# A decode layer's feed-forward tail: GELU, up and w_down taken out of the hand-synchronised section

## The chip, the core and the metric

The kernel runs on one core of one Trainium2 chip. A core has five engines with a queue of instructions each: TensorE (PE, matrix products), VectorE (DVE), ScalarE (ACT), GpSimd (POOL) and SyncE (SP), which here issues nearly all transfers. Sixteen DMA engines move data between the device memory (HBM) and the two on-chip memories' larger one, SBUF; matrix products land in PSUM, eight banks of 2 KB in each of 128 partitions. The metric is the time of one execution in microseconds, as the device measures it, median of the runs. The profiled execution is one further run whose instructions were recorded.

## The reference

One token goes through one layer of a transformer: layernorm, attention over a cache of 65,536 positions with 4 key/value heads and 32 query heads of 128, an output projection with a residual, and then a gated feed-forward block. Everything is bf16 in memory.

```python
def _A_ref(x, k_cache, v_cache, wq, wo):            # k_cache, v_cache: (1, 4, 65536, 128)
    q = (x @ wq).reshape(B, Sq, 32, 128)...
    p = _softmax(einsum("bhqd,bhkd->bhqk", q, k) * Dh ** -0.5, axis=-1)
    return einsum("bhqk,bhkd->bhqd", p, v)... @ wo  # wq: (1024, 4096), wo: (4096, 1024)

def _B_ref(x, w_gate, w_up, w_down):                # (1024, 3584), (1024, 3584), (3584, 1024)
    return (_gelu(x @ w_gate) * (x @ w_up)) @ w_down

x = A_x
h = x + _A_ref(_layernorm(x), A_k_cache, A_v_cache, A_wq, A_wo)
h2 = h + _B_ref(_layernorm(h), B_w_gate, B_w_up, B_w_down)
```

`_gelu` is the tanh approximation. The two caches are 134 MB; the weights of the feed-forward block are 7.3 MB each, 22 MB in all.

## The kernel before

All large data pass through one ring of four slots in SBUF (`ring`, 4 MB each; `slot(i, n)` is `n` slots from slot `i` on). The attention loop uses slots 2 and 3 for keys and 0 and 1 for values; after it, `wo` comes into slots 2 and 3, `w_gate` into 0 and 1 and `w_up` into 2 and 3. `w_down`'s 3584 rows are dealt out as 28 groups of 128 rows, one row of each group in each partition. The first FA = 16 groups (`wa`, 4 MB) overwrite slot 0, the next eight (`wb`, 2 MB) overwrite slot 1, and the last FZ = 4 groups have memory of their own, `w_end` (768 KB for three groups and 256 KB for the last). The first two take the place of `w_gate`, so they can be loaded only when gate's matmuls have read it. All these loads are issued by SyncE, on one DMA queue.

The feed-forward block goes in these steps. The normalised row stands in `hz` (8 columns of 128 values, each in a 32-wide tile of zeros). `ffn_in` (L557) loads a matrix and runs 64 matmuls (`wide_rows`, L325), eight for each column, four of them side by side in the four column groups of the array, into banks 0 and 1; VectorE transposes the two banks so that the 3584 results stand as 28 columns of 128 partitions (`rows_to_columns`, L332). This is done for gate, then GELU follows (L568 to L577: five small operations on VectorE around one Tanh on ScalarE, result `gl`), then the same for up, and `actz` gets gate times up (L600), each column in the middle of 63 zeros, so that a shifted 32-wide window puts the result on any row wanted.

The product with `w_down` accumulates in bank 2 and bank 7 (`d_ps`, `d_odd`). Its start value is the residual h: GpSimd spreads it out in `hb` (L585 to L589), and 16 fp32 matmuls put it into bank 2 (L590), half of which VectorE copies to bank 7 (L594). `wa`'s 16 groups are multiplied with 512 columns at a time into bank 6 (`down_wide`, L636, 32 matmuls); ScalarE copies that to SBUF and 8 matmuls add it to banks 2 and 7 (`add_wide`, L643). The other 12 groups go straight into banks 2 and 7, eight matmuls of 128 columns each (`down`, L621). Between the groups stand matmuls whose result nobody reads (`stay_busy`, L629). At the end VectorE and ScalarE copy rows 30 to 33 and 94 to 97 out and SyncE stores them (L669 to L672).

What sets the order? Nearly the whole kernel is written as a list of operations (`Flow`, L17), which `issue` (L82) turns into instructions with semaphores placed by hand; since `issue` makes every instruction, the profile gives them line 105. This list is issued inside a section (`tc.tile_critical`, L610), in which the framework (Tile) neither orders nor synchronises anything. Around a section the framework sets up an entry and an exit: SyncE lets the engines in; at the end each engine drains, SyncE waits for all of them (the join), and what depends on the section's data waits for that. Outside of sections the framework orders each engine's instructions itself, by their place in the text and by when it plans their inputs to be ready, and places the semaphores. An instruction that depends on nothing earlier can be put ahead of what precedes it in the text; `tc.keep_in_program_order` pins it behind the instruction before it on its engine. From L650 on, `tc.manual_schedule` keeps TensorE's instructions in the order of the text.

Before the change there are two sections. The first holds everything from the start to `actz`, and the loads of `wa` and `wb`. Outside stand the two loads of `w_end` (L613 to L619), pinned to their place, with semaphores of their own. The second section (L651 to L664) holds the filler, `wa`'s and `wb`'s groups and the fold; TensorE waits in it for the loads' semaphores. `w_end`'s groups stand outside again.

Of the kernel before, what the change touches and what calls it, by code (L numbers as in the profile page):

```python
# [8 lines left out]
ACT = mybir.ActivationFunctionType  # L9
ALU = mybir.AluOpType  # L10
# [108 lines left out]
def kernel(  # L119
# [13 lines left out]
    nc = tc.nc  # L133
    P = 128
    D = A_x.shape[-1]
# [4 lines left out]
    F = B_w_gate.shape[1]  # L140
    DC = D // P
    FC = F // P
# [11 lines left out]
    NT2 = Hkv * NH  # L154
    CW = DCH * CH * Dh
    NB = 512
# [25 lines left out]
    def sb(name, shape, dtype=F32):  # L182
        return const.tile(shape, dtype, name=name)
# [22 lines left out]
    def slot(i, n=1):  # L206
        return ring[:, i * CW:(i + n) * CW]
# [4 lines left out]
    s_qk, s_step = [tc.alloc_semaphore("from_pe_%d" % i) for i in range(2)]  # L212
    STEPS = 5
    k_sem = [tc.alloc_semaphore("k_landed_%d" % i) for i in range(DCH)]
    end_sem = [tc.alloc_semaphore("end_landed_%d" % i) for i in range(2)]


    XU = 32
# [106 lines left out]
    def wide_rows(banks, bkeys, rows_z, zkey, ci, blocks, wkeys, first, last):  # L325

        for t, w in enumerate(blocks):
            q = t % 4
            op("pe", "matmul", r=[zkey] + wkeys, w=[bkeys[t // 4]], out=banks[t // 4][32 * q:32 * q + 32, :], lhsT=rows_z[:, ci, :], rhs=w,
               start=first, stop=last, tile_position=(0, 32 * q))  # L330

    def rows_to_columns(banks, bkeys, key, order="p n -> p n", **sizes):  # L332

        w = [ps.shape[-1] for ps in banks]
        r = over(28672, [sum(w)])
        o = 0
        for ps, n, bk in zip(banks, w, bkeys):
            src = ps.rearrange(order, **sizes)
            op("dve", "transpose", r=[bk], w=[key], out=r[:, o:o + n].rearrange("p (e j) -> p e j", j=32) if sizes else r[:, o:o + n], in_=src)
            o += n  # L340
        return r[:, 0:o:32]
# [208 lines left out]
    def f_blocks(w_row):  # L550

        blocks = []
        for o, n in zip((0, P * FA), FW):
            blocks += [w_row[:, o + q * n:o + (q + 1) * n] for q in range(4)]
        return blocks

    def ffn_in(wmat, key, s0, b0):  # L557
        banks = [bank[b0 + i][:, 0:n] for i, n in enumerate(FW)]
        bkeys = ["B%d" % (b0 + i) for i in range(2)]
        rk = ["R%d" % s0, "R%d" % (s0 + 1)]  # L560
        wv = slot(s0, 2)[:, 0:DC * F].rearrange("p (c n) -> p c n", c=DC)
        f.dma("sp", wv, wmat.rearrange("(p c) n -> p c n", p=P), w=rk, sem=r_sem[s0], wait=[(s_step, STEPS * NT2 - 1)])
        for ci in range(DC):
            wide_rows(banks, bkeys, hz, "xz", ci, f_blocks(wv[:, ci, :]), rk, ci == 0, ci == DC - 1)
        return rows_to_columns(banks, bkeys, key, "p (j e) -> p e j", j=32)

    g_sb = ffn_in(B_w_gate, "g_r", 0, 0)
    t1 = sb("t1", [P, FC])  # L568
    op("dve", "tensor_tensor", r=["g_r"], w=["t1"], out=t1[:], in0=g_sb, in1=g_sb, op=ALU.mult)
    op("dve", "tensor_scalar", r=["t1"], w=["t1"], out=t1[:], in0=t1[:], scalar1=0.044715, scalar2=1.0, op0=ALU.mult, op1=ALU.add)  # L570
    op("dve", "tensor_tensor", r=["t1", "g_r"], w=["t1"], out=t1[:], in0=t1[:], in1=g_sb, op=ALU.mult)
    th = sb("th", [P, FC])
    op("act", "activation", r=["t1"], w=["th"], out=th[:], in_=t1[:], func=ACT.Tanh, scale=0.7978845608028654)
    hg = sb("hg", [P, FC])
    op("dve", "tensor_scalar", r=["g_r"], w=["hg"], out=hg[:], in0=g_sb, scalar1=0.5, scalar2=None, op0=ALU.mult)
    gl = sb("gl", [P, FC])
    op("dve", "scalar_tensor_tensor", r=["th", "hg"], w=["gl"], out=gl[:], in0=th[:], scalar=1.0, in1=hg[:], op0=ALU.add, op1=ALU.mult)  # L577


    OR = 8  # L580
    OB = D // OR
    orow = [30, 94, 31, 95, 32, 96, 33, 97]
    d_ps = bank[2][:, 0:OB]
    op("dve", "memset", w=["B2"], ap=d_ps, constant=0.0)
    hb = over(10240, [DC, P])  # L585
    op("pool", "memset", w=["hb"], ap=hb, constant=0.0)
    op("pool", "tensor_tensor", r=["h_col", "o_of"], w=["hb"], out=hb.rearrange("p j (b m) -> p j m b", b=2)[:, :, orow[0]:orow[0] + OR // 2, :],
       in0=h_col[:].unsqueeze(2).unsqueeze(3).to_broadcast([P, DC, OR // 2, 2]),
       in1=o_of[:].rearrange("p (a b) -> p a b", b=2).unsqueeze(1).to_broadcast([P, DC, OR // 2, 2]), op=ALU.mult)  # L589
    for j in range(DC):  # L590
        op("pe", "matmul", r=["hb", "sel16"], w=["B2"], out=d_ps[:, j:OB:DC], lhsT=hb[:, j, :], rhs=sel16[:],
           start=False, stop=False, skip_group_check=True)
    d_odd = bank[7][:, 0:OB]
    op("dve", "tensor_copy", r=["B2"], w=["B7"], out=d_odd[64:P, :], in_=d_ps[64:P, :])  # L594

    AZ = 31
    actz = over(16384, [FC, 2 * AZ + 2], BF16)
    op("pool", "memset", w=["actz"], ap=actz, constant=0.0)
    u_r = ffn_in(B_w_up, "u_r", 2, 0)
    op("dve", "tensor_tensor", r=["u_r", "gl", "actz"], w=["actz"], out=actz[:, :, AZ], in0=u_r, in1=gl[:], op=ALU.mult)  # L600

    wa = slot(0)[:, 0:FA * D].rearrange("p (e n) -> p e n", e=FA)
    wb = slot(1)[:, 0:FB * D].rearrange("p (e n) -> p e n", e=FB)
    wb_src = B_w_down[P * FA:F, :].rearrange("(p e) n -> p e n", p=P)
    parts = [(wa, 0, FA, f.dma("sp", wa, B_w_down[0:P * FA, :].rearrange("(p e) n -> p e n", p=P), after=["R0"], inc=(r_sem[0], 16)), r_sem[0])]
    e0 = 0
    w_body = wb_src[:, e0:FB - FZ, :]
    part = wb[:, e0:FB - FZ, :]
    parts.append((part, FA + e0, FB - FZ - e0, f.dma("sp", part, w_body, after=["R1"], inc=(r_sem[1], 16)), r_sem[1]))
    with tc.tile_critical(no_gpsimd_drain=True):  # L610
        f.issue()

    ends = []  # L613
    for i, (e1, e2) in enumerate(((FB - FZ, FB - 1), (FB - 1, FB))):
        d = nc.sync.dma_start(out=w_end[:, e1 - FB + FZ:e2 - FB + FZ, :], in_=wb_src[:, e1:e2, :])
        d.then_inc(end_sem[i], 16)
        tc.no_tile_sem_insts.add(d.ins.name)
        tc.keep_in_program_order(d)
        ends.append((d, e1, e2))  # L619

    def down(a_row, w_row, landed=None):  # L621
        for j in (0, 4, 1, 5, 2, 6, 3, 7):
            q, m = divmod(orow[j], 32)
            mm = nc.tensor.matmul((d_ps, d_odd)[q // 2][32 * q:32 * q + 32, :], lhsT=a_row[:, AZ - m:AZ - m + 32], rhs=w_row[:, j * OB:(j + 1) * OB],  # L624
                             start=False, stop=False, skip_group_check=True, tile_position=(0, 32 * q))
            if landed is not None:
                tc.declare_no_dep(mm.ins, landed.ins, query=mybir.DependencyQuery.ANY, reason="TensorE waits for the load's own semaphore ahead of it")

    def stay_busy(n):  # L629
        for i in range(n):  # L630
            nc.tensor.matmul(bank[5][:], lhsT=qs[:, 0, 0, 0:P], rhs=qs[:, 1 + i % 3].rearrange("p s c -> p (s c)")[:, 0:NB], start=True, stop=True)
# [4 lines left out]
    def down_wide(a_row, w_row, e, n):  # L636
        for h in range(DS):
            q = 2 * (e % 2) + h
            mm = nc.tensor.matmul(e_ps[32 * q:32 * q + 32, :], lhsT=a_row[:, AZ:AZ + 32], rhs=w_row[:, h * NB:(h + 1) * NB],
                             start=(e < 2), stop=(e >= n - 2), tile_position=(0, 32 * q))  # L640
        return mm

    def add_wide():  # L643
        for c in range(C4):
# [1 line left out]
            nc.tensor.matmul((d_ps, d_odd)[h][64 * h:64 * h + 64, :], lhsT=fold[:, 1 - c // 2:65 - c // 2], rhs=e_sb[:, c * OB:(c + 1) * OB],  # L646
                             start=False, stop=False, skip_group_check=True, tile_position=(0, 64 * h))

    (w_rows, a0, n, at, sem), (w_rows2, a2, n2, at2, sem2) = parts
    ctx.enter_context(tc.manual_schedule(engines={mybir.EngineType.PE}))  # L650
    with tc.tile_critical(no_gpsimd_drain=True):  # L651
        stay_busy(4)
        nc.tensor.wait_ge(sem, at)
        for e in range(n):
            mm = down_wide(actz[:, a0 + e, :], w_rows[:, e, :], e, n)
        mm.then_inc(s_step, 1)
        nc.scalar.wait_ge(s_step, STEPS * NT2 + 1)
        nc.scalar.copy(out=e_sb[:], in_=e_ps[:]).then_inc(from_act, 1)
        stay_busy(3)
        nc.tensor.wait_ge(from_act, 1)  # L660
        add_wide()
        nc.tensor.wait_ge(sem2, at2)
        for e in range(n2):
            down(actz[:, a2 + e, :], w_rows2[:, e, :])  # L664
    for i, (d, e1, e2) in enumerate(ends):
        nc.tensor.wait_ge(end_sem[i], 16)
        for e in range(e1, e2):
            down(actz[:, FA + e, :], w_end[:, e - FB + FZ, :], d)
    h2 = sb("h2", [P, 2, OB], BF16)  # L669
    nc.vector.tensor_copy(out=h2[0:64, 0, :], in_=d_ps[0:64, :])  # L670
    nc.scalar.copy(out=h2[0:64, 1, :], in_=d_odd[64:P, :])  # L671
# [31 lines left out]
```

## Time and profile before

| what | value |
|---|---|
| time, median of 3 runs (lowest, highest) | 409.39 us (409.34, 409.49) |
| profiled execution: its own time | 409.36 us |
| profiled execution: span from first to last instruction | 407.6 us |
| read from HBM | 173.02 MB, 424 GB/s over the span |
| DMA queue of SyncE, share of 16 engines | 98.6% |
| busy: PE, DVE, ACT, POOL | 56%, 49%, 10%, 4% |
| mean granted TensorE clock | 0.803 |

Times in the profile are microseconds from the first instruction. In a line of the chain or of the instructions in order of time, the first figure is the start and the second the length; "out<-in" names what is written and read, "x64" is the number of instructions merged in the line, and the bracket gives the idle time of the engine before it and what ended it. SPq is SyncE's queue, which issues transfers. "Time to landing" runs from a transfer's issue to the semaphore that says that all of it has arrived. In a table of stretches each engine has its busy time and, in brackets, its instructions; after the engines come the granted TensorE clock (1.00 is full), the share of the DMA engines and GB/s.

### The profile page before, as it was taken

How to read it: one execution, taken by the hardware profiler on the slowest of the kernel's cores; microseconds unless marked ns; L12 is line 12 of the kernel's file. 1: busy time of each engine (PE TensorE's matmuls, PEld its weight loads, DVE VectorE, ACT ScalarE, POOL GpSimd, SP SyncE). 2: the span in 40 equal slices, each digit the busy share in tenths (PEclk: the TensorE clock that was granted, in tenths of full speed). 3: DMA queues.
4: the chain of work that ended last, by engine and by line, in shares of the span. 5: the costliest groups of instructions: out<-in, count | busy, mean ns of one | idle time of the engine just before them, and what ended most of it. 6: DMA issues, size and time to landing. Idle time of an engine off the chain costs nothing. (4 is left out here: it accounts for less than half of the span.)

```text
span 407.6 us, 3713 instructions
## 1 busy us (share of the span) xinstructions
PE 227.4 (56%) x1557; PEld 100.0 (25%) x1558; DVE 201.0 (49%) x160; ACT 40.0 (10%) x142; POOL 16.6 (4%) x27
## 2 busy tenths in 40 slices
PE   0432854674677468715873686468456737634156
PEld 0110322231232133202321332233122213222123
DVE  2226860894079328734962686188509940121110
ACT  1000003000300130030003000300040021000000
POOL 4210000001000000010000001000000000030000
PEclk9975896899569778968896689589968986566688
DMA  8999999999999999999999999999999999999995
GB/s 360 412 453 420 441 434 418 453 418 432 434 460 418 412 445 469 418 412 418 495 418 389 441 431 447 412 466 412 418 450 457 424 405 428 457 445 435 396 415 220
DMA packets 4958, 173.10 MB, mean 425 GB/s; under 512 B 596, under 2 KB 600, under 8 KB 856
## 3 DMA queue, kind: packets, MB, share of 16 engines
q1 hardware_dynamic: 4904, 173.02, 98.6%
q8 instruction: 4, 0.07, 0.1%
q14 instruction: 2, 0.02, 0.0%
q10 hardware_dynamic: 48, 0.00, 0.0%
HBM read 173.02 MB, written 0.00 MB: 424 GB/s over the span
## 5 line engine op out<-in xcount | busy, mean ns | idle before, releaser
L105 DVE STREAM_TRANSPOSE ktb<-ring 128x4096 f32<-128x4096 f32 x32 | 141.1, 4417 | 74.9 <-DMA ring<-in_A_k_cache_dram 74.9
L450 PE MATMUL bank<-ktb,qs 128*128 128x512 bf16 x512 | 129.6, 412 | 55.1 <-PEq L436 55.1
L450 PEld LDWEIGHTS bank<-ktb,qs 128*128 128x128 bf16 x512 | 51.0, 103 | 130.5 <-issue 83.2
L462 PE MATMUL bank<-ring,pt 128*32 128x512 bf16 x512 | 44.8, 527 | 36.5 <-PEq L436 36.5
L105 ACT ACTIVATE pt<-sc,nb 128x256 bf16<-128x256 f32 x64 | 31.5, 494 | 256.6 <-DVE nb L105 256.6
L105 DVE STREAM_TRANSPOSE sc<-bank 128x512 f32<-128x512 f32 x32 | 22.2, 695 | 35.9 <-PE bank L450 35.9
L462 PEld LDWEIGHTS bank<-ring,pt 128*32 128x32 bf16 x512 | 18.9, 127 | 59.3 <-issue 55.6
L105 PE MATMUL bank<-ring,xz 128*32 128x512 bf16 (+1 forms) x192 | 16.6, 521 | 22.6 <-DMA ring<-in_B_w_gate_dram 8.3
L105 DVE STREAM_TRANSPOSE ktb<-bank 128x512 f32<-128x512 f32 (+1 forms) x6 | 4.0, 672 | 34.3 <-PE bank L105 34.0
L105 DVE TENSOR_REDUCE mx<-sc 128x8 f32<-128x2048 f32 x8 | 18.3, 2286 | 0.3
L454 PE MATMUL bank<-ident_f,mx 128*8 128x128 f32 x8 | 2.5, 307 | 25.8 <-PEq L436 25.8
L105 POOL COPY qs<-qsel 128x512 bf16<-128x512 bf16 x4 | 5.3, 1326 | 233.6 <-PE bank L450 219.6
L105 PEld LDWEIGHTS bank<-ring,xz 128*32 128x32 bf16 x192 | 6.5, 128 | 31.3 <-issue 14.5
L105 ACT ACTIVATION_READ_ACCUMULATOR pt<-sc,nb 128x1 f32 x64 | 12.0, 187 | 0.0
L471 PE MATMUL bank<-sel,acc_sb 128*128 128x8 f32 x64 | 8.2, 255 | 6.2 <-PEq L436 6.2
L471 PEld LDWEIGHTS bank<-sel,acc_sb 128*128 128x128 f32 x64 | 7.7, 191 | 10.0 <-issue 10.0
L105 ACT COPY acc_sb<-bank 128x512 f32<-128x512 f32 x8 | 4.7, 586 | 47.4 <-PE bank L462 47.4
L105 PE MATMUL bank<-ring,ktb 128*32 128x512 bf16 x64 | 7.0, 614 | 1.9 <-DMA ring<-in_A_wo_dram 1.2
L454 PEld LDWEIGHTS bank<-ident_f,mx 128*8 128x8 f32 x8 | 0.7, 83 | 29.5 <-issue 29.5
L456 PE MATMUL bank<-diag,ones_f 8*128 8x8 f32 x16 | 3.5, 287 | 5.7 <-PEq L436 5.7
L105 POOL MEMSET ktb<- 128x1024 bf16 (+2 forms) x3 | 3.5, 1164 | 74.9 <-PE bank L450 74.9
L105 DVE TENSOR_TENSOR h_col<-bank,x_col 128x8 f32<-128x8 f32 x1 | 0.2, 167 | 11.4 <-PE bank L105 11.4
(96 smaller groups left out, 61.4 us busy)
## 6 DMA issues: line engine op xcount, KB each, us to landing
ring<-in_A_k_cache_dram SPq DMA_DIRECT2D x16, 4096.0 KB, 24.8
ring<-in_A_wq_dram SPq DMA_DIRECT2D x2, 4096.0 KB, 16.5
ring<-in_A_wo_dram SPq DMA_DIRECT2D x2, 4096.0 KB, 25.5
ring<-in_B_w_gate_dram SPq DMA_DIRECT2D x1, 7168.0 KB, 26.6
ring<-in_B_w_up_dram SPq DMA_DIRECT2D x1, 7168.0 KB, 30.4
ring<-in_B_w_down_dram SPq DMA_DIRECT2D x1, 4096.0 KB, 21.8
ring<-in_B_w_down_dram SPq DMA_DIRECT2D x1, 2048.0 KB, 26.3
w_end<-in_B_w_down_dram SPq DMA_DIRECT2D x1, 768.0 KB, 27.5
```

The source lines that it names most:

```text
L105: ins = getattr(self.eng[e], o["call"])(**o["kw"])
L450: m = nc.tensor.matmul(bank[c][:], lhsT=qs[:, jt].rearrange("p s c -> p (s c)")[:, s * P:(s + 1) * P], rhs=mv[:, :, J, :, u], start=(s == ...
L454: nc.tensor.transpose(out=mxT_ps, in_=mx1[:], identity=ident_f[:]).then_inc(s_step, 1)
L456: nc.tensor.matmul(bc_ps, lhsT=ones_f[0:rep, :], rhs=diag[:], start=True, stop=True).then_inc(s_step, 1)
L462: m = nc.tensor.matmul(acc[32 * q:32 * q + 32, :], lhsT=pt[:, c, n, :, :].rearrange("p h s -> p (h s)"), rhs=v_sb[:, c, :, n, :], start=(c ...
L471: m = nc.tensor.matmul(o_ps, lhsT=acc_sb[:, u * Dh:(u + 1) * Dh], rhs=sel[:, u:SQ:NS], start=(u == 0), stop=(u == NS - 1))
```

## The change

The first section ends with gate's matmuls. The load of `w_up` stays in it, behind gate's (`ffn_load`). What follows stands outside of sections: the four loads of `w_down` in the order `wa`, `wb`, first and second `w_end`, each with a semaphore of its own (`end_sem` has four now), none with a wait or a signal of the framework's, and none pinned to its place; the operations on h; GELU; up's matmuls; and all of `w_down`'s groups. The loads form a group with a fence on TensorE (`waits_itself`), so that the framework lets TensorE read what they bring without waiting; TensorE waits by `wait_ge` on the loads' semaphores instead. Since up's load was issued in the section, TensorE's wait for its landing stands in a small section of its own. The memory views, the sizes and the matmuls are the same. The filler is four matmuls behind up's, as before, and two instead of three while ScalarE copies `wa`'s result.

```diff
-    def ffn_in(wmat, key, s0, b0):
+    def ffn_load(wmat, s0):
         ...
-        return rows_to_columns(banks, bkeys, key, "p (j e) -> p e j", j=32)
+        return wv, rk
+
+    f_banks = [bank[i][:, 0:n] for i, n in enumerate(FW)]
+    gate_w, rk = ffn_load(B_w_gate, 0)
+    for ci in range(DC):
+        wide_rows(f_banks, ["B0", "B1"], hz, "xz", ci, f_blocks(gate_w[:, ci, :]), rk, ci == 0, ci == DC - 1)
+    up_w, _ = ffn_load(B_w_up, 2)
+    with tc.tile_critical(no_gpsimd_drain=True):
+        f.issue()
+
+    ctx.enter_context(tc.manual_schedule(engines={mybir.EngineType.PE}))
     ...
+    loads = [(wa, B_w_down[0:P * FA, :].rearrange("(p e) n -> p e n", p=P)), (wb[:, 0:FM, :], wb_src[:, 0:FM, :]),
+             (w_end[:, 0:FZ - 1, :], wb_src[:, FM:FB - 1, :]), (w_end[:, FZ - 1:FZ, :], wb_src[:, FB - 1:FB, :])]
+    for (dst, src), sem in zip(loads, end_sem):
+        d = nc.sync.dma_start(out=dst, in_=src)
+        d.then_inc(sem, 16)
+        tc.no_tile_sem_insts.add(d.ins.name)
+        tc.add_to_no_dep_group("loads", d.ins)
+    waits_itself = nc.tensor.nop()
+    tc.declare_fence(waits_itself.ins, group="loads")
     ...
-    parts = [(wa, 0, FA, f.dma("sp", wa, B_w_down[0:P * FA, :].rearrange("(p e) n -> p e n", p=P), after=["R0"], inc=(r_sem[0], 16)), r_sem[0])]
     ...
-    with tc.tile_critical(no_gpsimd_drain=True):
-        f.issue()
-
-    ends = []
-    for i, (e1, e2) in enumerate(((FB - FZ, FB - 1), (FB - 1, FB))):
-        d = nc.sync.dma_start(out=w_end[:, e1 - FB + FZ:e2 - FB + FZ, :], in_=wb_src[:, e1:e2, :])
-        d.then_inc(end_sem[i], 16)
-        tc.no_tile_sem_insts.add(d.ins.name)
-        tc.keep_in_program_order(d)
-        ends.append((d, e1, e2))
     ...
+    nc.gpsimd.memset(hb, 0.0)
+    nc.gpsimd.tensor_tensor(out=hb..., in0=h_col..., in1=o_of..., op=ALU.mult)
+    nc.gpsimd.memset(actz, 0.0)
     ...
+    nc.vector.memset(d_ps, 0.0)
+    g_sb = columns(over(28672, [sum(FW)]))
     ...
+    for j in range(DC):
+        nc.tensor.matmul(d_ps[:, j:OB:DC], lhsT=hb[:, j, :], rhs=sel16[:], start=False, stop=False, skip_group_check=True)
+    d_odd = bank[7][:, 0:OB]
+    nc.vector.tensor_copy(out=d_odd[64:P, :], in_=d_ps[64:P, :])
+
     with tc.tile_critical(no_gpsimd_drain=True):
+        nc.tensor.wait_ge(r_sem[2], f.landed[r_sem[2].name])
+    for ci in range(DC):
+        ...
+    u_r = columns(over(28672, [sum(FW)]))
+    nc.vector.tensor_tensor(out=actz[:, :, AZ], in0=u_r, in1=gl[:], op=ALU.mult)
     ...
-    (w_rows, a0, n, at, sem), (w_rows2, a2, n2, at2, sem2) = parts
-    ctx.enter_context(tc.manual_schedule(engines={mybir.EngineType.PE}))
-    with tc.tile_critical(no_gpsimd_drain=True):
-        stay_busy(4)
-        nc.tensor.wait_ge(sem, at)
     ...
-    for i, (d, e1, e2) in enumerate(ends):
-        nc.tensor.wait_ge(end_sem[i], 16)
-        for e in range(e1, e2):
-            down(actz[:, FA + e, :], w_end[:, e - FB + FZ, :], d)
+    stay_busy(4)
+    nc.tensor.wait_ge(end_sem[0], 16)
+    for e in range(FA):
+        down_wide(actz[:, e, :], wa[:, e, :], e, FA)
+    nc.scalar.copy(out=e_sb[:], in_=e_ps[:])
+    stay_busy(2)
+    add_wide()
+    e = FA
+    for (dst, _), sem in list(zip(loads, end_sem))[1:]:
+        nc.tensor.wait_ge(sem, 16)
+        for i in range(dst.shape[1]):
+            down(actz[:, e, :], dst[:, i, :])
+            e += 1
```

More of the change, by code (lines that the diff above doesn't have):

```diff
@@ L214 @@
     k_sem = [tc.alloc_semaphore("k_landed_%d" % i) for i in range(DCH)]
-    end_sem = [tc.alloc_semaphore("end_landed_%d" % i) for i in range(2)]
+    end_sem = [tc.alloc_semaphore("end_landed_%d" % i) for i in range(4)]
     XU = 32
@@ L555, in f_blocks @@
         return blocks
-    def ffn_in(wmat, key, s0, b0):
-        banks = [bank[b0 + i][:, 0:n] for i, n in enumerate(FW)]
-        bkeys = ["B%d" % (b0 + i) for i in range(2)]
+    def ffn_load(wmat, s0):
         rk = ["R%d" % s0, "R%d" % (s0 + 1)]
@@ L562, in ffn_in @@
         f.dma("sp", wv, wmat.rearrange("(p c) n -> p c n", p=P), w=rk, sem=r_sem[s0], wait=[(s_step, STEPS * NT2 - 1)])
-        for ci in range(DC):
-            wide_rows(banks, bkeys, hz, "xz", ci, f_blocks(wv[:, ci, :]), rk, ci == 0, ci == DC - 1)
-        return rows_to_columns(banks, bkeys, key, "p (j e) -> p e j", j=32)
[L567 to L577, printed above, removed]
+        return wv, rk
[7 more added lines that the diff above has]
+    ctx.enter_context(tc.manual_schedule(engines={mybir.EngineType.PE}))
+    wa = slot(0)[:, 0:FA * D].rearrange("p (e n) -> p e n", e=FA)
+    wb = slot(1)[:, 0:FB * D].rearrange("p (e n) -> p e n", e=FB)
+    wb_src = B_w_down[P * FA:F, :].rearrange("(p e) n -> p e n", p=P)
+    FM = FB - FZ
+    loads = [(wa, B_w_down[0:P * FA, :].rearrange("(p e) n -> p e n", p=P)), (wb[:, 0:FM, :], wb_src[:, 0:FM, :]),
[7 more added lines that the diff above has]
+    tc.declare_fence(waits_itself.ins, group="loads")
     OR = 8
@@ L583 @@
     d_ps = bank[2][:, 0:OB]
-    op("dve", "memset", w=["B2"], ap=d_ps, constant=0.0)
     hb = over(10240, [DC, P])
[L586 to L594, printed above, removed]
     AZ = 31
     actz = over(16384, [FC, 2 * AZ + 2], BF16)
-    op("pool", "memset", w=["actz"], ap=actz, constant=0.0)
-    u_r = ffn_in(B_w_up, "u_r", 2, 0)
-    op("dve", "tensor_tensor", r=["u_r", "gl", "actz"], w=["actz"], out=actz[:, :, AZ], in0=u_r, in1=gl[:], op=ALU.mult)
@@ L602 @@
-    wa = slot(0)[:, 0:FA * D].rearrange("p (e n) -> p e n", e=FA)
-    wb = slot(1)[:, 0:FB * D].rearrange("p (e n) -> p e n", e=FB)
-    wb_src = B_w_down[P * FA:F, :].rearrange("(p e) n -> p e n", p=P)
-    parts = [(wa, 0, FA, f.dma("sp", wa, B_w_down[0:P * FA, :].rearrange("(p e) n -> p e n", p=P), after=["R0"], inc=(r_sem[0], 16)), r_sem[0])]
[L606 to L609, printed above, removed]
@@ L610 @@
-    with tc.tile_critical(no_gpsimd_drain=True):
-        f.issue()
-    ends = []
-    for i, (e1, e2) in enumerate(((FB - FZ, FB - 1), (FB - 1, FB))):
-        d = nc.sync.dma_start(out=w_end[:, e1 - FB + FZ:e2 - FB + FZ, :], in_=wb_src[:, e1:e2, :])
-        d.then_inc(end_sem[i], 16)
-        tc.no_tile_sem_insts.add(d.ins.name)
-        tc.keep_in_program_order(d)
-        ends.append((d, e1, e2))
-    def down(a_row, w_row, landed=None):
+    nc.gpsimd.memset(hb, 0.0)
+    nc.gpsimd.tensor_tensor(out=hb.rearrange("p j (b m) -> p j m b", b=2)[:, :, orow[0]:orow[0] + OR // 2, :],
+                            in0=h_col[:].unsqueeze(2).unsqueeze(3).to_broadcast([P, DC, OR // 2, 2]),
+                            in1=o_of[:].rearrange("p (a b) -> p a b", b=2).unsqueeze(1).to_broadcast([P, DC, OR // 2, 2]), op=ALU.mult)
@@ new lines, with columns @@
+    nc.gpsimd.memset(actz, 0.0)
+    def columns(r):
+        o = 0
+        for ps, n in zip(f_banks, FW):
+            nc.vector.transpose(out=r[:, o:o + n].rearrange("p (e j) -> p e j", j=32), in_=ps.rearrange("p (j e) -> p e j", j=32))
+            o += n
+        return r[:, 0:o:32]
+    nc.vector.memset(d_ps, 0.0)
+    g_sb = columns(over(28672, [sum(FW)]))
+    t1, th, hg, gl = [sb(n, [P, FC]) for n in ("t1", "th", "hg", "gl")]
+    nc.vector.tensor_tensor(out=t1[:], in0=g_sb, in1=g_sb, op=ALU.mult)
@@ new lines @@
+    nc.vector.tensor_scalar(out=t1[:], in0=t1[:], scalar1=0.044715, scalar2=1.0, op0=ALU.mult, op1=ALU.add)
+    nc.vector.tensor_tensor(out=t1[:], in0=t1[:], in1=g_sb, op=ALU.mult)
+    nc.scalar.activation(out=th[:], in_=t1[:], func=ACT.Tanh, scale=0.7978845608028654)
+    nc.vector.tensor_scalar(out=hg[:], in0=g_sb, scalar1=0.5, scalar2=None, op0=ALU.mult)
+    nc.vector.scalar_tensor_tensor(out=gl[:], in0=th[:], scalar=1.0, in1=hg[:], op0=ALU.add, op1=ALU.mult)
+    for j in range(DC):
+        nc.tensor.matmul(d_ps[:, j:OB:DC], lhsT=hb[:, j, :], rhs=sel16[:], start=False, stop=False, skip_group_check=True)
@@ new lines @@
+    d_odd = bank[7][:, 0:OB]
+    nc.vector.tensor_copy(out=d_odd[64:P, :], in_=d_ps[64:P, :])
+    with tc.tile_critical(no_gpsimd_drain=True):
+        nc.tensor.wait_ge(r_sem[2], f.landed[r_sem[2].name])
+    for ci in range(DC):
+        for t, w in enumerate(f_blocks(up_w[:, ci, :])):
+            q = t % 4
+            nc.tensor.matmul(f_banks[t // 4][32 * q:32 * q + 32, :], lhsT=hz[:, ci, :], rhs=w, start=(ci == 0), stop=(ci == DC - 1),
+                             tile_position=(0, 32 * q))
@@ L622, in down @@
+    u_r = columns(over(28672, [sum(FW)]))
+    nc.vector.tensor_tensor(out=actz[:, :, AZ], in0=u_r, in1=gl[:], op=ALU.mult)
+    def down(a_row, w_row):
         for j in (0, 4, 1, 5, 2, 6, 3, 7):
             q, m = divmod(orow[j], 32)
-            mm = nc.tensor.matmul((d_ps, d_odd)[q // 2][32 * q:32 * q + 32, :], lhsT=a_row[:, AZ - m:AZ - m + 32], rhs=w_row[:, j * OB:(j + 1) * OB],
+            nc.tensor.matmul((d_ps, d_odd)[q // 2][32 * q:32 * q + 32, :], lhsT=a_row[:, AZ - m:AZ - m + 32], rhs=w_row[:, j * OB:(j + 1) * OB],
@@ L625, in down @@
                              start=False, stop=False, skip_group_check=True, tile_position=(0, 32 * q))
-            if landed is not None:
-                tc.declare_no_dep(mm.ins, landed.ins, query=mybir.DependencyQuery.ANY, reason="TensorE waits for the load's own semaphore ahead of it")
     def stay_busy(n):
@@ L638, in down_wide @@
             q = 2 * (e % 2) + h
-            mm = nc.tensor.matmul(e_ps[32 * q:32 * q + 32, :], lhsT=a_row[:, AZ:AZ + 32], rhs=w_row[:, h * NB:(h + 1) * NB],
+            nc.tensor.matmul(e_ps[32 * q:32 * q + 32, :], lhsT=a_row[:, AZ:AZ + 32], rhs=w_row[:, h * NB:(h + 1) * NB],
                              start=(e < 2), stop=(e >= n - 2), tile_position=(0, 32 * q))
-        return mm
     def add_wide():
@@ L647, in add_wide @@
                              start=False, stop=False, skip_group_check=True, tile_position=(0, 64 * h))
-    (w_rows, a0, n, at, sem), (w_rows2, a2, n2, at2, sem2) = parts
-    ctx.enter_context(tc.manual_schedule(engines={mybir.EngineType.PE}))
-    with tc.tile_critical(no_gpsimd_drain=True):
-        stay_busy(4)
-        nc.tensor.wait_ge(sem, at)
[L654 to L664, printed above, removed]
-    for i, (d, e1, e2) in enumerate(ends):
-        nc.tensor.wait_ge(end_sem[i], 16)
-        for e in range(e1, e2):
-            down(actz[:, FA + e, :], w_end[:, e - FB + FZ, :], d)
+    stay_busy(4)
[11 more added lines that the diff above has]
+            e += 1
     h2 = sb("h2", [P, 2, OB], BF16)
```

## The prediction

> **What bounds the kernel now.** I read the page's strip of DMA load first, then the chain that ended last, then SyncE's own instructions and waits, then TensorE's instructions in order of time for the last 20 us, and last the stretches with the granted clock.
>
> ```profile
> DMA  8999999999999999999999999999999999999995
> q1 hardware_dynamic: 4904, 173.02, 98.6%
> ```
>
> The DMA engines hold work from start to end, on one queue (98.6% of the span). The time is therefore the bytes, plus what is left to do after the last byte. The chain shows that rest:
>
> ```profile
> 344.09 26.63 DMA ring<-in_B_w_gate_dram
> ...
> 376.66 27.47 DMA w_end<-in_B_w_down_dram
> 404.13 0.14 issue
> 404.27 0.52 PE bank L624 x24
> 404.79 0.01 issue
> 404.79 0.35 PE bank L624 x8
> 405.14 0.02 issue
> 405.17 0.26 ACT h L671
> ```
>
> Only the last 1 MB of w_down (`w_end`, two loads) has matmuls behind its landing, and they are few: 24, then 8. PE ends at 405.14, 0.35 us after the last landing.
>
> ```profile
> 375.61 0.81 SPq L105 DMA_DIRECT2D ring<-in_B_w_down_dram  x2
> 376.66 18.16 SPq L615 DMA_DIRECT2D w_end<-in_B_w_down_dram  x2
> SPq L610 <- DVEq L610: 17.3, 1, 17.3
> ```
>
> The first two lines are SyncE's, the third its waits. The four w_down loads leave in the order `wa`, `wb`, first `w_end`, second `w_end`. The two `w_end` issues lie 17.8 us apart (376.66 and 394.49): between them SyncE sits 17.3 us in the join that ends the section, waiting for VectorE. So a load that depends on nothing in the section was put ahead of the section's join, and the next one behind it.
>
> ```profile
> 387.70 4.82 PE L105 MATMUL bank<-ring,xz 128*32 128x512 bf16 x64 [7.46 <-DMA ring<-in_B_w_up_dram]
> 395.47 0.81 PE L631 MATMUL bank<-qs 128*128 128x512 bf16 x3 [2.95 <-SPq L651]
> 397.41 3.24 PE L639 MATMUL bank<-ring,ktb 128*32 128x512 bf16 x32 [1.13 <-DMA ring<-in_B_w_down_dram]
> 400.58 1.14 PE L631 MATMUL bank<-qs 128*128 128x512 bf16 x3
> 401.65 0.66 PE L646 MATMUL bank<-e_sb,fold 128*64 128x128 f32 x8
> 402.31 1.08 PE L624 MATMUL bank<-ring,ktb 128*32 128x128 bf16 x64
> 404.27 0.82 PE L624 MATMUL bank<-w_end,ktb 128*32 128x128 bf16 x32 [0.88 <-DMA w_end<-in_B_w_down_dram]
> ```
>
> This is the staircase of landings that TensorE follows. From issue plus time to landing: up 387.7 (357.27 + 30.4), `wa` 397.41 (375.61 + 21.8), `wb` 402.28 (375.98 + 26.3), `w_end` 404.13 and 404.79 (394.49 + 10.3). PE waits at each step, so it has slack everywhere but after the last byte.
>
> **The change part by part**, on the profiled execution (span 407.6, its own time 409.36, against the median 409.39 of the three runs).
>
> The section now ends after gate's last matmul (375.59), not after VectorE's `actz` (394.20). The old end gives the price of a join: from VectorE's end to the next load 0.29 us (394.49), to TensorE's next instruction 1.04 us (395.24). So `wa` and `wb` leave at about 375.9 to 376.4 instead of 375.61 and 375.98. Queued behind the join on SyncE are these two loads and the entry of the next section. The up load keeps the queue fed until 387.69; cover 11 us; cost 0.
>
> GELU on VectorE starts at 376.6 (375.59 + 1.04) instead of 375.45: memset 0.17, transposes 1.40, six small operations and Tanh about 1.2, done near 379.4. GpSimd's two memsets and one product (0.95 + 0.31 + 1.59 us), which ran from 363.3 under gate's load, now start after the join and end by 379.5. The 16 fp32 matmuls of h (1.96 us) end by 379.9, the copy (0.31) by 380.2. If the two engines were made to take turns on the shared tile, everything ends near 383. All of it lies under up's landing; cover 4.7 to 7.5 us; cost 0. One more table load on ScalarE (1.28 us, the one row of its kind) would also fit.
>
> The new section around the wait for up has an entry and an exit. The nearest rows are that 1.04 us hop, and the 0.85 us between 403.39 and 404.24 at the old second section's end, which a landing ended. From nothing to 1.9 us, then; I take 1.04, the row that no landing cut short. Up then ends near 393.6 and `actz` near 395.2, against `wa`'s landing at 397.41: cover 2.2 us, and 1.3 at the upper end. Cost 0.
>
> TensorE's filler: four now directly behind up, then two instead of three (0.38 us each). They end before `wa` lands, and the fold waits for ScalarE's copy (401.27) anyway. The second section's end goes; the idle time there (403.39 to 404.24) was ended by `w_end`'s landing, so this gains 0 to 0.1.
>
> The loads are what is left. All four lose their pin to program order. `wa` and `wb` overwrite slots that gate's matmuls read, so they stay behind the join. The two `w_end` loads write memory that nothing earlier touches, so nothing holds them behind `wa`. They may go into the gap ahead of the join, which on SyncE now opens right after up's issue (357.6), or ahead of the whole section. Either way their 1 MB moves in front of `wa`. The queue's bytes and end stay the same (404.79), but the order of landing changes. The last 1 MB took 2.51 us (404.79 - 402.28), so `wa` lands at 399.92 and `wb` is the last to land, at 404.79. `wa`'s rows end at 403.16 (3.24), the copy at 403.78 (0.04 + 0.58), the fold at 404.44 to 404.8 (0.66, with or without the 0.37 that lay ahead of it): just hidden. Behind the last byte there are now 64 + 32 matmuls instead of 8. The rate is (1.08 - 0.22)/63 = 13.7 ns in the first group and (0.52 - 0.22)/23 = 13.0 in the second, 0.22 us being one matmul's length. With 13.5 ns: 95 x 13.5 + 220 = 1.50 us, so PE ends at 406.29 instead of 405.14: **+1.15 us, 410.5**. The ends for this case: 13.0 ns a matmul and none lost at the switch gives +1.1; 17 ns (1.08/64, with each group's latency counted again) +1.5.
>
> The clock: the stretches show where it stands as the staircase ends.
>
> ```profile
> 394.50:397.90 3.40, 1.30 (x15) 0.57 (x20) 0.00 (x0) 0.00 (x0) 0.00 (x0) 0.99 0.94 400
> 397.90:401.30 3.40, 3.40 (x30) 1.11 (x23) 0.00 (x0) 0.58 (x1) 0.00 (x0) 0.51 0.96 402
> 401.30:404.70 3.40, 2.52 (x98) 1.69 (x96) 0.00 (x0) 0.00 (x0) 0.00 (x0) 1.00 0.47 186
> ```
>
> The seventh figure after the length is the granted clock. 1.30 us of work in 3.4 us led to half clock in the next stretch, 3.40 us of work to full clock again. The filler now comes right behind up, so TensorE idles from about 394.5 to 399.9 and starts `wa`'s rows cold, as it mostly does now (0.51). By 404.8 it has worked 403.2 - 399.9 and the fold, so I take full clock for the tail.
>
> [...]
>
> **The rivals.** First, order kept: the framework issues the loads as written, `w_end` last. Then the landings stay and PE ends at 405.14; with both `w_end` loads landed before 404.79 at best 0.2 us less. 409.4, no change. For it: the second `w_end` load did leave behind the join. Against it: the first did not, and the old text pinned both to their place. It decides as soon as neither `w_end` load passes `wa`.
>
> Second, only one passes, as now: the gap took one load. Then `wb` lands at 404.13, and from 404.27 96 matmuls take 1.50: 405.77, +0.63, 410.0.
>
> Third, TensorE late or cold. Cold: 96 matmuls at 27 ns from 404.8, +2.45, 411.8. Late: `wa` and `wb` behind the new section's join in SyncE's queue would leave after up's landing, near 388.2; with some 1.7 us to the first bytes (the output's store, issued at 405.49 in a span that ends at 407.6, bounds it) the queue stands empty 2.2 us, 411.6. For: SyncE takes joins in order. Against: the loads come first in the text and are ready 11 us earlier.
>
> Fourth, faster: in stretches of 0.6 us from 402.4 the DMA share falls to 0.54, 0.30, 0.16 and 0.01, as some engines finish early; 0.6 x (0.46 + 0.70 + 0.84 + 0.99) = 1.8 us of idle share. If another order of sizes levelled this, 407.6. No row shows that the order sets it.
>
> **How the numbers follow.** Both loads ahead 0.38 (410.5; own range 410.3 to 410.9), one ahead 0.12 (410.0), order kept 0.28 (409.4), late or cold 0.14 (411.6 to 411.8), faster 0.08. A measurement of this kernel can tell about 0.2%, 0.8 us. Slower: 0.38 + 0.13, and a quarter of the one-ahead case, 0.54. Same: 0.28, the rest of one ahead and a little of the late case, 0.38. Faster 0.08. The range from 409.1 (order kept, with 0.2 gained) to 411.8 (cold) leaves out the faster case and a little above. The forecast is 410.5.
>
> **What would show it.** In SyncE's list both `w_end` issues ahead of `wa`'s, near 358 or near 1; `wa`'s rows start near 399.9; the last chain ends in `wb`'s landing with some 96 short matmuls behind it. In the order kept, `w_end` still ends the chain with 24 and 8. It would be wrong if `wb` lands well before 404, if the idle time ahead of the last matmuls is put down to SyncE, or if the tail's clock reads 0.5.

## The result, and the profile after

The changed kernel takes 410.80 us (median of 6 runs, 410.65 to 411.91), the kernel before 409.34 us in the same comparison (6 runs, 409.26 to 409.49). The ratio is 1.0040 with a 95% interval of 1.0027 to 1.0053: slower by 0.4%, 1.46 us. The profiled execution's span is 409.0 us, against 407.6.

The first view is SyncE's instructions in order of time, at the start of the kernel and around the feed-forward block (start, length, what it issues).

```profile
0.81 0.40 SPq L172 DMA_DIRECT2D ring<-in_A_wq_dram  x1
1.32 0.83 SPq L579 DMA_DIRECT2D w_end<-in_B_w_down_dram  x2
2.36 0.37 SPq L105 DMA_DIRECT2D ring<-in_A_wq_dram  x1
...
346.77 0.33 SPq L105 DMA_DIRECT2D ring<-in_B_w_gate_dram  x1
359.94 0.33 SPq L105 DMA_DIRECT2D ring<-in_B_w_up_dram  x1
378.48 0.80 SPq L579 DMA_DIRECT2D ring<-in_B_w_down_dram  x2
```

Both `w_end` loads now leave at 1.32 us, second of all, ahead of the second half of the query weights. They start at 1.3 and 1.8 us, and an instruction of SyncE at the section's entry (L568) runs between the two, at 1.7. Gate's load is issued 2.68 us later than before (346.77 against 344.09), near the 2.51 us that the last 1 MB took before the change. At the end only `wa` and `wb` are left to load, 0.27 us after gate's last matmul (378.21).

The chain that ended last, its end:

```profile
378.48 0.33 SPq L579
378.81 0.05 issue
378.86 25.96 DMA ring<-in_B_w_down_dram
404.82 0.04 issue
404.87 1.58 PE bank L633 x96
406.45 0.02 issue
406.47 0.26 ACT h L670
```

The last landing is at 404.82, where it was before (404.79). But what lands last is now `wb`, and 96 matmuls stand behind it where there were 8. PE ends at 406.45 instead of 405.14: 1.31 of the 1.4 us by which the span grew. TensorE's own list says the same:

```profile
390.91 4.58 PE L625 MATMUL bank<-ring,xz 128*32 128x512 bf16 x64 [7.67 <-PEq L620]
395.42 1.04 PE L638 MATMUL bank<-qs 128*128 128x512 bf16 x4
400.11 3.22 PE L646 MATMUL bank<-ring,ktb 128*32 128x512 bf16 x32 [3.65 <-DMA ring<-in_B_w_down_dram]
403.26 0.94 PE L638 MATMUL bank<-qs 128*128 128x512 bf16 x2
404.12 0.66 PE L652 MATMUL bank<-e_sb,fold 128*64 128x128 f32 x8
404.87 1.08 PE L633 MATMUL bank<-ring,ktb 128*32 128x128 bf16 x64
405.77 0.62 PE L633 MATMUL bank<-w_end,ktb 128*32 128x128 bf16 x32
```

The new section's exit shows in the bracket of the first line: up landed at 390.24 (359.94 + 30.3), its matmuls began 0.67 us later. That is hidden, as `actz` was done at 396.94 and `wa` landed at 399.98.

### The profile page after: what moved, and what is told of

Read it like the earlier page. It is cut to its first block, busy times and chain, and to the rows that moved or that the text cites. A ratio compares the mean times of both kernels' runs of the same rounds, so it can differ in the third digit from the quotient of the medians.

```text
span 409.0 us, 3707 instructions
## 1 busy us (share of the span) xinstructions
PE 228.5 (56%) x1557; PEld 100.6 (25%) x1557; DVE 200.8 (49%) x160; ACT 40.0 (10%) x142; POOL 16.7 (4%) x27
## 3 DMA queue, kind: packets, MB, share of 16 engines
q1 hardware_dynamic: 4904, 173.02, 98.3%
## 5 line engine op out<-in xcount | busy, mean ns | idle before, releaser
L105 PEld LDWEIGHTS bank<-ring,xz 128*32 128x32 bf16 x128 | 4.4, 129 | 23.2 <-issue 12.7
L602 DVE STREAM_TRANSPOSE ktb<-bank 128x512 f32<-128x512 f32 (+1 forms) x4 | 2.3, 618 | 11.8 <-PE bank L625 11.8
L105 DVE STREAM_TRANSPOSE ktb<-bank 128x512 f32<-128x512 f32 x2 | 1.4, 716 | 12.9 <-PE bank L105 12.7
## 6 DMA issues: line engine op xcount, KB each, us to landing
ring<-in_B_w_up_dram SPq DMA_DIRECT2D x1, 7168.0 KB, 30.3
```

The costliest lines, as they stand in the source:

```text
L105: ins = getattr(self.eng[e], o["call"])(**o["kw"])
L602: nc.vector.transpose(out=r[:, o:o + n].rearrange("p (e j) -> p e j", j=32), in_=ps.rearrange("p (j e) -> p e j", j=32))
```

## The experiments

Theory A: nothing counts but the order of landing, that is, how many matmuls stand behind the last byte. Theory B: the sections, joins and semaphores of the new arrangement cost the time. Theory C: the 1 MB at the front delays the attention loop. The experiments also take up the clock, which the prediction had left as a rival. Every median stands beside the kernel before on the same chip (409.36 or 409.37).

**e1, the new arrangement with the old order of loads.**

```diff
         tc.add_to_no_dep_group("loads", d.ins)
+        tc.keep_in_program_order(d)
```

> The changed kernel with all four loads pinned to the order of the text (wa, wb, w_end, w_end); nothing else differs. Theory A (the changed order of landing leaves 96 matmuls instead of 8 behind the last byte, and nothing else counts): the chain ends again in w_end's landing with 24 and 8 matmuls, PE ends 0.35 us behind the last landing, 409.3 to 409.5. Theory B (the framework's sections, joins and semaphores around TensorE's wait cost the time): still 410.6 to 410.9. Theory C (1 MB ahead of the query weights delays the attention loop): 409.3 to 409.5, as A.

Measured: 409.40 (ratio 1.0001, 0.9992 to 1.0010). The whole difference is gone with one line that changes only the loads' place in SyncE's queue. B falls: the new sections, the join after gate and the framework's own semaphores are all still there. One detail came out otherwise than expected. The chain ends in the first `w_end` load, and the matmuls behind it ran at half clock (the third figure from the end of the stretch below, where 1.00 is full):

```profile
378.18 25.92 DMA w_end<-in_B_w_down_dram
404.10 0.04 issue
404.14 1.10 PE bank L634 x26
```

```profile
404.10:405.30 1.20, 1.05 (x32) 0.71 (x32) 0.07 (x1) 0.03 (x1) 0.00 (x0) 0.50 0.01 5
```

With so few matmuls behind the last landing it hardly matters: TensorE ends at 405.25 instead of 405.14.

**e2, the old arrangement with the new order.** The kernel before, without its pins.

```diff
         tc.no_tile_sem_insts.add(d.ins.name)
-        tc.keep_in_program_order(d)
         ends.append((d, e1, e2))
```

> The kernel before with the pin of its two w_end loads taken away; its two sections and all else stay. Theory A: the loads float ahead of everything, wb lands last, near 404.8, and 96 matmuls follow it: 410.5 to 410.9. Theory B: 409.3 to 409.5, since the sections are the old ones. Theory C: 410.5 to 410.9, as A.

Measured: 411.23 (ratio 1.0045, 1.0031 to 1.0058), slower than A's 410.5 to 410.9. TensorE's list from e2 shows where the rest lies:

```profile
399.99 3.61 PE L638 MATMUL bank<-ring,ktb 128*32 128x512 bf16 x32 [0.53 <-DMA ring<-in_B_w_down_dram]
403.53 1.08 PE L630 MATMUL bank<-qs 128*128 128x512 bf16 x3
404.54 0.66 PE L645 MATMUL bank<-e_sb,fold 128*64 128x128 f32 x8
405.13 1.08 PE L623 MATMUL bank<-ring,ktb 128*32 128x128 bf16 x64
406.46 0.63 PE L623 MATMUL bank<-w_end,ktb 128*32 128x128 bf16 x32 [0.25 <-SPq L650]
```

With 1 MB ahead, `wa`'s rows start 2.6 us later than before the change; the fold now ends after `wb` has landed, so the 64 matmuls start at 405.13 instead of 404.87. Then TensorE stands idle for 0.25 us in the second section's join, and with the matmuls' drain ahead of it 1.33 us lie between the two starts, against 0.90 in the changed kernel. The join was there before the change too, under `w_end`'s landing. PE ends at 407.14, 0.69 us later than in the changed kernel: 0.26 from the late fold, 0.43 from the join. So with this order the old arrangement is the slower one.

**e3, one load early.** Only the first `w_end` load may float.

```diff
-    for (dst, src), sem in zip(loads, end_sem):
+    for i in (2, 0, 1, 3):
+        (dst, src), sem = loads[i], end_sem[i]
...
+        if i != 2:
+            tc.keep_in_program_order(d)
```

> The changed kernel with only the first w_end load (768 KB) free to float; the other three are pinned in the order wa, wb, second w_end. Theory A: wb lands 0.66 us ahead of the end of the stream, 96 matmuls at 13.5 ns follow it, PE ends 0.6 us later than before, 409.9 to 410.1. Theory B: 410.6 to 410.9. Theory C: three quarters of the 1.46 us, 410.4.

Measured: 410.22 (ratio 1.0026, 1.0014 to 1.0037), 0.86 above before, 0.12 above A's range and 0.18 below C's figure; six of the seven runs lie between 410.13 and 410.52, one at 411.10. Its chain:

```profile
378.73 25.64 DMA ring<-in_B_w_down_dram
404.37 0.04 issue
404.42 1.58 PE bank L636 x96
406.00 0.02 issue
```

The 96 matmuls took the same 1.58 us as in the changed kernel; `wb` landed 0.45 us earlier than there, not 0.66. PE ends 0.86 us later than before, which is all of the measured difference, so A's account holds, with the landing put too early and the tail too short.

**e4 and e5, the 1 MB stays early but less stands behind the last byte.** In e4 `wb` comes in two loads of 7 and 1 groups, and `w_end`'s 32 matmuls are done ahead of `wa`'s. In e5 `wb` comes in 4, 2, 1 and 1.

`rows(i)` waits for load i and runs its groups' matmuls. The diff of e4, and the line of e5 that differs:

```diff
-             (wb[:, 0:FM, :], wb_src[:, 0:FM, :]),
+             (wb[:, 0:FM - 1, :], wb_src[:, 0:FM - 1, :]), (wb[:, FM - 1:FM, :], wb_src[:, FM - 1:FM, :]),
...
     stay_busy(4)
+    rows(3)
+    rows(4)
     nc.tensor.wait_ge(end_sem[0], 16)
...
     add_wide()
...
+    rows(1)
+    rows(2)
```

```diff
+             *[(wb[:, u:v, :], wb_src[:, u:v, :]) for u, v in ((0, 4), (4, 6), (6, 7), (7, 8))],
```

> The changed kernel with both w_end loads still ahead of everything, but wb loaded in two pieces of seven groups and one group, and w_end's 32 matmuls done ahead of wa's. Behind the last landing are 8 matmuls, as before the change. Theory A: 409.3 to 409.6, though the early 1 MB stays early. Theory B: 410.6 to 410.9. Theory C: 410.6 to 410.9.

> As e4, both w_end loads ahead of everything and their matmuls ahead of wa's, but wb now lands in four pieces of 4, 2, 1 and 1 groups, so that no piece has more than its own few matmuls behind its landing. In e4 the 56 matmuls of the seven-group piece started at 404.37 and pushed the last 8 out to 405.50. Theory A (only matmuls behind the last landings count): PE ends near 405.15 and the time is 409.2 to 409.5. Theory C (the early 1 MB itself costs what was left in e4, 0.37 us): 409.7 to 409.9.

Measured: e4 409.73 (ratio 1.0012, 1.0003 to 1.0021), e5 409.77 (1.0010, 1.0001 to 1.0018). Three quarters of the loss go without moving the early loads back, which C as the main cause does not allow; but 0.4 us stay. That is above A's range in both, by 0.13 and 0.27 us, and e5 lies in the range that C had for what was left. In e4 I had a reason ready: 56 matmuls start at 404.37 and push the last 8 to 405.50. e5 takes that reason away and keeps the 0.4. Its chain:

```profile
381.94 23.11 DMA ring<-in_B_w_down_dram
405.05 0.04 issue
405.09 0.35 PE bank L633 x8
```

Exactly 8 matmuls and 0.35 us, as before the change, but the last landing is 405.05 instead of 404.79. That left two suspects for the later landing, the early 1 MB and the small pieces.

**e9, the same small pieces with nothing early.** The `w_end` loads are pinned right behind `wa` and used behind its rows.

```diff
-    for (dst, src), sem in zip(loads, end_sem):
+    for i in (0, 5, 6, 1, 2, 3, 4):
+        (dst, src), sem = loads[i], end_sem[i]
...
+        tc.keep_in_program_order(d)
```

> As e5 (wb in pieces of 4, 2, 1 and 1 groups, the last one 256 KB), but the two w_end loads are pinned right behind wa and used behind its rows, so nothing is issued at the front of the kernel. Behind the last landing stand the same 8 matmuls. If the early 1 MB cost the 0.41 us that e5 kept (theory C): 409.3 to 409.5. If the small pieces at the end of the stream cost it: 409.7 to 409.9.

Measured: 409.67 (ratio 1.0007, 0.9998 to 1.0016), 0.03 below the range for small pieces and 0.17 above the one for C, the last landing at 404.95:

```profile
379.39 25.57 DMA ring<-in_B_w_down_dram
404.95 0.04 issue
405.00 0.35 PE bank L635 x8
```

About 0.30 of the 0.41 us stays with nothing issued early, though e9's interval reaches no difference at all; what is left for C is about 0.1 us, no more than these runs can tell. C falls as the main cause. That the small pieces are what costs the 0.3 us is likely and not shown, since the last landing can come as late without them: e10 below, with the changed kernel's loads, has it at 404.99. Cutting the end of the stream into small loads gains nothing, as far as these runs go.

**e6, the clock: no filler.** Both `stay_busy` calls of the changed kernel are taken out.

```diff
-    stay_busy(4)
     nc.tensor.wait_ge(end_sem[0], 16)
...
-    stay_busy(2)
     add_wide()
```

> The changed kernel without any filler matmul (neither the four behind up nor the two beside ScalarE's copy; their result is read by nobody). Theory A: wa's own rows, 3.2 us of work, bring the clock back by the time of the last 96 matmuls: 410.6 to 411.0, as the changed kernel. Cold rival: the tail reads a granted clock of 0.5 and 96 matmuls take 27 ns instead of 13.5: 411.8 to 412.1.

Measured: 412.39 (ratio 1.0066, 1.0053 to 1.0078), above A's range by 1.4 us and above the cold rival's by 0.3. Five runs lie between 412.37 and 412.56, one at 410.73. A stretch of e6 over the tail, and the same of the changed kernel (length, PE's busy time, ..., then the clock as the third figure from the end):

```profile
404.80:408.50 3.70, 3.39 (x104) 2.79 (x100) 0.27 (x1) 0.23 (x1) 0.00 (x0) 0.50 0.00 0
```

```profile
404.80:406.50 1.70, 1.52 (x96) 1.35 (x96) 0.07 (x1) 0.03 (x1) 0.00 (x0) 1.00 0.00 0
```

At half clock the 96 matmuls run from 405.44 to 408.25, 2.81 us instead of 1.58, and they start 0.57 us later, behind a fold that took 1.12 us instead of 0.66. That later start is what the cold rival had left out. Ahead of `wa`'s rows TensorE idles equally long in both kernels, from 396.5 to 400.1. But in e6 the clock fell during that idle time (0.88 over 396.7 to 400.0), in the changed kernel only after the rows had begun (1.00 over 396.6 to 400.1). In the changed kernel TensorE then worked from 400.11 to 404.78 without a break, the filler beside ScalarE's copy included, and the clock was full again by 404.2. In e6 it stood idle for 0.68 us beside the copy, and the clock stayed at 0.50 to the end. That this break is what kept it down is a reading of two profiles. What the times show is the price of leaving the filler out: five runs of six above 412.3 here, none of six in the changed kernel. Why one run in six escaped the loss is not shown, as no profile of that run was taken.

**e10, more filler.** Fourteen instead of four behind up.

```diff
-    stay_busy(4)
+    stay_busy(14)
```

> The changed kernel with fourteen filler matmuls behind up instead of four, which end before wa lands; their result is read by nobody. If the clock of the tail is what spreads the changed kernel's times (one run of six at 411.91) and e6's (412.4): wa's rows and the 96 matmuls run at full clock in every run, 410.6 to 410.9 and no run above 411.2. If the spread has another cause: single runs near 411.9 again.

Measured: 410.84 (ratio 1.0040, 1.0026 to 1.0053), runs from 410.68 to 410.88 and one at 411.64. In the profiled execution `wa`'s rows run at full clock (1.00 from 400.1 to 403.4) and take 1.91 us instead of 3.22, and it gains nothing:

```profile
400.27 1.91 PE L646 MATMUL bank<-ring,ktb 128*32 128x512 bf16 x32 [1.52 <-DMA ring<-in_B_w_down_dram]
402.12 0.60 PE L638 MATMUL bank<-qs 128*128 128x512 bf16 x2
402.87 0.66 PE L652 MATMUL bank<-e_sb,fold 128*64 128x128 f32 x8
405.03 1.08 PE L633 MATMUL bank<-ring,ktb 128*32 128x128 bf16 x64 [1.51 <-DMA ring<-in_B_w_down_dram]
```

The time saved turns into 1.51 us of waiting for `wb`. I had expected no such single run as the one at 411.64, had the clock been its cause; but no run shows that fourteen filler matmuls secure the clock. Each run has its mean granted clock on record. The changed kernel's run at 411.91 has 0.792 where the other five have 0.800 to 0.816, and the run at 411.64 here has 0.786 where the others have 0.808 to 0.816; e3's single high run has 0.786 against 0.804 to 0.816. The excess of these runs, 1.2, 0.9 and 0.9 us, is near the 1.23 us by which e6's 96 matmuls were longer at half clock. A cold tail fits all this. It isn't shown, as no profile of those runs was taken and the mean doesn't say where in the kernel the clock was low.

**e11, no filler with the old order.** The pinned kernel e1 without any filler.

```diff
-    stay_busy(4)
...
-    stay_busy(2)
```

> The pinned kernel (e1) without any filler. The tail reads 0.5 in the stretches, as in e6. Theory A: with the landings in the old order the half clock falls on work that waits for landings, and only 8 to 32 matmuls show it: 409.4 to 409.9, against 1.6 us of loss without filler where 96 matmuls stand behind the last byte. If the clock costs the same wherever the landings stand: 411.

Measured: 409.67 (ratio 1.0008, 0.9999 to 1.0017), 0.3 above, in an interval that just reaches no difference, with runs from 409.35 to 410.21. The profiled execution was one of the quickest (409.35) and its tail ran at full clock (1.00 from 401.0 to 405.4), so the half clock that I expected in it was not seen there. In e1, with the filler, the tail had read 0.50. So with this order the profiles do not tie the tail's clock to the filler, and what makes the 0.3 us is not shown. The medians still say what was asked: without filler the old order loses at most some 0.3 us, the new one 1.6.

**e7 and e8, TensorE held back.** The pinned kernel with filler between up's landing and up's first matmul, eight in e7 and forty in e8.

```diff
         nc.tensor.wait_ge(r_sem[2], f.landed[r_sem[2].name])
+    stay_busy(8)
```

> The pinned kernel (e1) with eight filler matmuls between up's landing and up's first matmul, some 3.4 us at half clock. In e1 the inputs of wa's rows were ready 2.0 us before wa landed, the fold ended 1.6 us before wb landed, and wb's rows ended 0.8 us before w_end landed. Theory A (TensorE follows the landings and is not the bound): 409.3 to 409.8. If TensorE, or the boundary around its wait, were the bound: 412.8.

> As e7 with forty filler matmuls: 8 at half clock (0.43 us) and 32 at full (0.215 us), 10.3 us, less some 1.5 us that up's matmuls gain from a warm clock. Theory A: the slack of about 4.4 us is used up and the rest shows: 412.5 to 414.5. If the slack is larger than I read it: below 411; if there is none: 418.

Measured: e7 409.46 (ratio 1.0001, 0.9992 to 1.0010), e8 413.25 (1.0099, 1.0084 to 1.0114). In e7 TensorE loses 3.1 us ahead of up's matmuls and starts `wa`'s rows 0.23 us later than e1 did; the rest of the staircase does not move:

```profile
388.80 3.19 PE L626 MATMUL bank<-qs 128*128 128x512 bf16 x7 [8.36 <-PEq L621]
391.92 4.28 PE L632 MATMUL bank<-ring,xz 128*32 128x512 bf16 x64
396.35 0.81 PE L626 MATMUL bank<-qs 128*128 128x512 bf16 x3 [0.16 <-issue]
397.71 1.91 PE L649 MATMUL bank<-ring,ktb 128*32 128x512 bf16 x32 [0.55 <-DVE ktb L635]
```

With forty, the chain that ended last no longer passes through the w_down loads: it runs from up's landing through the filler (9.98 us from 388.99, where 10.3 was expected from an estimate of 8 matmuls at half clock and 32 at full, a split that no view of e8 shows), up's matmuls, VectorE and all that TensorE does behind them. So a delay of 0.67 us at up's start, which is what the new section costs, is free, and the slack ends between 3 and 10 us.

## Why the prediction was right, point by point

**The mechanism.** The forecast was that both `w_end` loads pass `wa`, so that `wb` lands last with 96 matmuls behind it. The profile after shows this, and e1 and e2 show it from both sides: pinning the loads undoes the change's cost in the new arrangement, and taking the pins away brings it in the old one.

**The size.** 410.5 was forecast and 410.80 measured, +1.15 against +1.46. The landing was to be at 404.79 (404.82) and `wa`'s at 399.92 (399.98). The one term that was too small is the tail: 95 steps of 13.5 ns and one length gave 1.50, measured 1.58 from a start 0.08 later; the end of PE is 1.31 later instead of 1.15. Another 0.09 lies between PE's end and the span's (2.55 us against 2.46); what is left, 0.06 us, is less than the runs of one kernel differ by.

**Where the loads would go.** I named two places, the gap ahead of the join (near 358) and the front (near 1). It was the front; why the framework chose it no run shows. For the time this made no difference, as the text said.

**What was costed at nothing.** The join after gate: `wa` left 0.27 us behind gate's last matmul, 0.29 was taken. GELU was done at 381.8 and the matmuls of h at 383.2, 7 us before up landed. GpSimd's three operations came in another order than the text's (the clearing of `actz` ahead of the product), also under that cover. The section around up's wait: 0.67 us, 1.04 was taken; e7 shows that it is free.

**The clock.** I took full clock for the tail because `wa`'s rows and the fold would be work enough. In the profiled execution it was so (1.00 from 404.2 on), but e6 shows that the reason was incomplete: the same rows and fold without the six filler matmuls left the tail at half clock in the profiled run (0.50 from 404.8 to 408.5), and five runs of six lost 1.6 us. I had costed the filler only as time in TensorE's queue. Nor is the filler a guarantee: e1, with the same filler, shows the last 32 matmuls at half clock (0.50, 1.05 us). That the forecast escaped the cold rival's 411.8 was in this part luck. That rival's 27 ns a matmul was an estimate, twice the 13.5 ns read before the change; from 404.8 it made 2.79 us of the tail, and e6's took 2.81 at 0.50. The rows also did not start cold, as I had it: they began at full clock, which fell to half between 400.1 and 401.3 (0.69 over that stretch, 0.50 behind it) and was back ahead of the tail.

**Misread lines.** TensorE's idle time ahead of `wa`'s rows was put at 394.5 to 399.9, some 5.4 us. The filler ran to 396.46 and 3.65 us was measured, against 1.13 before the change. TensorE was said to wait at each step of the staircase; at `wb`'s it did not, as those matmuls start at 402.31 straight behind the fold, 0.03 us behind the landing. The granted clock is the sixth figure behind the length of a stretch, not the seventh, and GELU has five operations on VectorE, not six. None of these is a term of the sum.

**The rivals.** Order kept: this is e1, 409.40 against 409.4 forecast for it. One ahead: e3, 410.22 against 410.0; `wb` landed at 404.37 where I had 404.13, and the tail was the same 0.08 longer. Late: the loads did not wait behind the new section, so no run shows the 1.7 us to the first bytes that was taken for it (before the change the DMA engines were first busy at 1.8, 1.0 us after the queue's first issue at 0.80), and in the pinned kernel a delay of TensorE by 3.1 us did not show (e7) where one of 10 us did (e8). Faster by a levelled end: with 2 MB as the last load the DMA share in the last stretches fell in the same way (0.44, 0.26, 0.13 and 0.00 in stretches of 0.6 us from 402.4, against 0.54, 0.30, 0.16 and 0.01), so this other order of sizes did not level it.

## What to carry to other kernels

Here the DMA queue took 98.6% of the 16 engines' span before the change and 98.3% after it, and the time was the stream, whose last byte landed at 404.79 and 404.82, plus the work behind it, 0.35 and 1.63 us of TensorE. In a kernel with a queue as full, read from the chain which load lands last and count the instructions that need it, before looking at anything else. When a load is handed to a framework that orders instructions, ask what holds it in its place: the two `w_end` loads, which depend on nothing, went to 1.32 us at the front, and another, larger load, the 2 MB of `wb`, became the last one. One line that pins the loads, without any other change, decided the whole difference here (409.40 against 410.80).

## What the runs showed that was not expected

Small loads at the end of the stream did not help. With the last 2 MB in pieces down to 256 KB, and the same 8 matmuls behind the last one, the times were 0.3 to 0.4 us higher (e9, e5). Their last landings, 404.95 and 405.05, came later than the 404.79 and 404.82 before and after the change, but e10's 404.99 without such pieces says that single profiles don't separate the two.

Taking out six matmuls whose result nobody reads cost 1.6 us where 96 matmuls stood behind the last byte, and some 0.3 us, at the edge of what the runs can tell, where 8 did. More filler than that bought nothing: `wa`'s rows ran 1.3 us faster and TensorE waited 1.5 us longer.
